# Weight conversions pinned behind a layer's stores, copies and maxima, with loads two units ahead

## The chip, the cores and the metric

The kernel runs on one core of a Trainium2 chip. The metric is device time in microseconds (us). Engines are named as in the profile: PE multiplies matrices (PEld is its weight load), DVE, ACT and POOL are the vector, scalar and general engines, and SP issues all transfers (its queue is SPq in the trace). Each engine takes its instructions in the order in which they stand in its queue.

## The reference

The program chains three parts over 2304 tokens (4 batches of 576): attention with a decay mask and no softmax, a feed-forward layer whose hidden value is the maximum of three products, and a gated one.

```python
rel = pos[:, None] - pos[None, :]
Dmat = np.where(rel >= 0, gamma[:, None, None] ** rel[None, :, :], 0.0)
x = np.matmul(scale * np.matmul(q, k.transpose(0, 1, 3, 2)) * Dmat, v)   # 4 x 8 heads, 576, 64
x = x.transpose(0, 2, 1, 3).reshape(2304, 512)
h = np.maximum(np.maximum(x @ w1, x @ w2), x @ w3)                       # 2304 x 768
y = h @ w_out                                                           # 2304 x 512
g = y @ w_gate                                                          # 2304 x 1536
out = (g * (1.0 / (1.0 + np.exp(-g))) * (y @ w_val)) @ w_out2           # 2304 x 512
```

q, k and v are float32. The weights arrive as 64-bit floats, which the kernel reads as pairs of 32-bit words and converts itself.

## The kernel before

**The main loop.** Lines 329 to 350 run 32 steps (n = 0 to 31), one for each batch, half sequence and pair of heads. A step loads the attention input of step n + 4 (`a_load`, L139 and L147, twelve transfers in later steps), finishes the attention of step n (`a_value`: the matmuls at L230 and L233, the copy L236 on ACT, the subtraction L237 on DVE), and prepares the next ones (`a_state`, `a_score`, `a_prep`, which transposes the loaded tile qk on DVE at L174 and L175). From step 4 on it also works on slices of the first feed-forward layer: `f_some` takes slices off a list, three in steps up to 8 and five from step 9 on.

**A slice** (`f_slice`) is twelve matmuls (L298) into a PSUM tile of 288 columns, of which there are two (`ps_mm`). Three slices belong to one block of h: the first is copied out by ACT (L302), the second and third are combined into it by DVE (the maxima, L304), and after the third SP stores the block to memory (L306, h_d).

**The conversions.** The 18 weight units of the first layer are converted in steps 1 to 8 (`win_conv`). The other weights, 42 units of 128 x 512, are converted from step 9 on by `spill`: SP loads a unit (`load_w`, 512 KB; L97 or L99; three buffers w), ACT takes both words (L106, L107), DVE puts them together (L108, L109, L110), and SP stores the result as float32 (L285, wd). The code calls `spill` once in each step from 9 on and a second time in steps 12, 16, 20, 24 and 28, that is 28 times, then 6 times in the loop at L382 (which finishes the slices of the last block and splits w_out into high and low parts, `wo_load`, and h, `h_split`), and 8 times in the loop at L456, which computes y = h w_out (matmuls L473, drained by L478 or L482). What needs the other weights, from L556 on, reads them from memory (`w_ops`, `p_ops`).

**What sets the order.** PE's instructions stand in the order of the code (`manual_schedule`). For ACT, DVE, POOL and SP a scheduler builds the queues: it goes through a simulated time line and puts in front what it holds ready first, so that a conversion, which depends only on its load and its buffers, may come many steps ahead of its place in the code. SP issues its transfers round-robin on eight semaphores, and a transfer waits until the one eight places before it has landed.

```python
        sp_load(i)
        sp_load(i + 1)
        l = conv32(sp_ld.pop(i))
```

Of the kernel before, what the change touches and what calls it, by code (L numbers as in the profile page):

```python
# [13 lines left out]
ACTF = mybir.ActivationFunctionType  # L14
ALU = mybir.AluOpType
# [47 lines left out]
def retention_moe(ctx, tc, consts, q, k, v, w1, w2, w3, w_out, w_gate, w_val, w_out2, out):  # L63
    nc = tc.nc
    pe, act, dve, pool, sp = nc.tensor, nc.scalar, nc.vector, nc.gpsimd, nc.sync

    def f(ap):
        return ap.bitcast(F32)

    dram = ctx.enter_context(tc.tile_pool(name="dram", bufs=1, space=DRAM))  # L70
    h_d = [dram.tile([F1, P, TOK[i][1]], F32, name=f"h_d{i}", tag=f"h_d{i}") for i in range(NHB)]
# [22 lines left out]
    def load_w(src):  # L94
        t = stg.tile([P, 512], U64, name="w64", tag="w64")
        if len(src.shape) == 3:
            sp.dma_start(out=t.rearrange("p (a b) -> p a b", a=src.shape[1]), in_=src)  # L97
        else:
            sp.dma_start(out=t, in_=src)  # L99
        return t  # L100

    def conv32(t):
        u = t.bitcast(U32).rearrange("p (n two) -> p n two", two=2)
        z = stg.tile([P, 512], U32, name="wz", tag="wz", bufs=2)
        l = stg.tile([P, 512], U32, name="wl", tag="wl")
        act.activation(f(z), f(u[:, :, 1]), ACTF.Copy, scale=float(2.0 ** -112))  # L106
        act.activation(l, u[:, :, 0], ACTF.Copy, scale=float(2.0 ** -29))  # L107
        dve.tensor_scalar(z, z, 3, None, ALU.logical_shift_left)  # L108
        dve.scalar_tensor_tensor(z, u[:, :, 1], 0x80000000, z, ALU.bitwise_and, ALU.bitwise_or)  # L109
        dve.tensor_tensor(l, z, l, ALU.add)  # L110
        return f(l)
# [16 lines left out]
    def a_load(n):  # L128
        if n >= NU:
            return  # L130
        b, h, pr = units[n]
        c0 = h * C
        u = {}
        for nm, s in (("k", k), ("q", q), ("v", v)):
            if nm == "q" and n >= PT:
                continue
            u[nm] = att.tile([CK, NC, 2, D], F32, name=f"{nm}n", tag=f"{nm}n", bufs=4)
            for e in range(2):
                sp.dma_start(out=u[nm][:, :, e, :],  # L139
                             in_=s[b, 2 * pr + e, c0:c0 + C].rearrange("(a p) d -> p a d", p=CK))  # L140
        if n >= PT:
            u["t"] = att.tile([P, 2, C // 32, 32], F32, name="qk", tag="qk", bufs=3)
            for i, s in enumerate((k, q)):
                for e in range(2):
                    for x in range(2):
                        g = 64 * e + 32 * x
                        sp.dma_start(out=u["t"][g:g + 32, i],  # L147
                                     in_=s[b, 2 * pr + e, c0:c0 + C, 32 * x:32 * x + 32].rearrange("(a p) d -> p a d", p=32))
        U[n] = u
# [71 lines left out]
    def a_value(n):  # L221
        b, h, pr = units[n]
        u = U.pop(n)
        z = stz[n % 3]
        o = psa.tile([P, C], F32, name="o_ps", tag="o_ps")
        for c in range(NC):
            for e in range(2):
                oc = o[64 * e:64 * e + 64, c * CK:(c + 1) * CK]
                if c or h:
                    pe.matmul(oc, z[:, c, e], u["qg"][:, c], start=c == 1 - h, stop=False, skip_group_check=True)  # L230
        for c in range(NC):
            for e in range(2):
                pe.matmul(o[64 * e:64 * e + 64, c * CK:(c + 1) * CK], u["v"][:, c, e], u["pT"][:, e, c],  # L233
                          start=False, stop=True, skip_group_check=True)
        xh, xl = [ffn.tile([P, C], F32R, name=f"x{x}", tag=f"x{x}{pr}", bufs=3) for x in "hl"]
        act.activation(xh, o, ACTF.Copy)  # L236
        dve.tensor_tensor(xl, o, f(xh), ALU.subtract)  # L237
        xs[(2 * b + h, pr)] = (xh, xl)
# [11 lines left out]
    def win_conv(i):  # L250
        if i >= len(win_units):
            return
        if i not in win_ld:
            win_load(i)
        win_load(i + 1)
        hi = ffn.tile([P, 512], F32R, name="wh", tag=f"wh{i}")
        lo = ffn.tile([P, 512], F32R, name="wlo", tag=f"wlo{i}")
        l = conv32(win_ld.pop(i))
        act.activation(hi, l, ACTF.Copy)
        pool.tensor_tensor(lo, l, f(hi), ALU.subtract)  # L260
        w_in[win_units[i]] = (hi, lo)


    sp_units = [(("o", fi), w_out[fi * P:fi * P + P, :]) for fi in range(F1)]
# [4 lines left out]
    sp_ld = {}  # L269
    sp_n = [0]  # L270

    def sp_load(i):
        if i < len(sp_units) and i not in sp_ld:
            sp_ld[i] = load_w(sp_units[i][1])

    def spill():
        i = sp_n[0]
        if i >= len(sp_units):
            return
        sp_n[0] += 1  # L280
        sp_load(i)
        sp_load(i + 1)
        l = conv32(sp_ld.pop(i))
        wd[sp_units[i][0]] = t = dram.tile([P, 512], F32, name=f"wd{i}", tag=f"wd{i}")
        sp.dma_start(out=t, in_=l)  # L285

    mx = {}

    def f_slice(hb, fi, wi):
        wh, wl = w_in[(fi, wi)]  # L290
        cw = TOK[hb][1]
        ps = ps_mm.tile([P, C], F32, name="ps", tag="mm")[:, 0:cw]
        n = 0
        for kc in range(KD):
            xh, xl = xs[(hb, kc)]
            ksl = slice(kc * P, kc * P + P)
            for l, r in ((wh, xl), (wl, xh), (wh, xh)):
                pe.matmul(ps, l[:, ksl], r, start=n == 0, stop=n == 3 * KD - 1)  # L298
                n += 1
        if wi == 0:  # L300
            mx[hb] = ffn.tile([P, C], F32, name="hmax", tag="hmax", bufs=3)[:, 0:cw]
            act.activation(mx[hb], ps, ACTF.Copy)  # L302
        else:
            dve.tensor_tensor(mx[hb], ps, mx[hb], ALU.max)  # L304
        if wi == 2:
            sp.dma_start(out=h_d[hb][fi], in_=mx[hb])  # L306

    fq = []

    def f_some(n):  # L310
        for _ in range(n):
            if fq:
                f_slice(*fq.pop(0))
# [15 lines left out]
    for n in range(NU):  # L329
        if n % NP == 0 and n:  # L330
            fq += [(n // NP - 1, fi, wi) for fi in range(F1) for wi in range(3)]
        a_load(n + 4)
        a_value(n)
        a_state(n + 1)
        a_score(n + 1)
        quota, ncv = ((2, 3) if n >= 9 else (1, 2)), 0
        if 1 <= n < 4:
            ncv = 1
        elif 4 <= n < 9:
            ncv = 3  # L340
        for _ in range(min(ncv, len(win_units) - wc)):
            win_conv(wc)
            wc += 1
        if n >= 9:
            spill()
            if n % 4 == 0:
                spill()
        f_some(quota[0])
        a_prep(n + 2)
        f_some(quota[1])  # L350
    pe_order.__exit__(None, None, None)
    psa_cm.__exit__(None, None, None)
    att_cm.__exit__(None, None, None)
# [99 lines left out]
        W[(nm, k)] = (hi, lo)  # L453


    for o in range(NHB):  # L456
        hb = order2[o]
        sb, blk, side = hb // 4, hb % 2, (hb // 2) % 2
        if sb == 0:
            if side == 0:  # L460
                x_tiles(blk)
                sc = [scratch() for j in range(KH)]
        else:
            st2 = wr.tile([P, 7, C], F32, name="sf", tag="sf")
        for e in (0, 2, 1, 3):
            ps = ps_mm.tile([P, C], F32, name="ps2", tag="mm")
            n = 0
            for fi in range(F1):
                wh, wl = wo[fi]
                hh, hl = hsp[(o, fi)]  # L470
                es = slice(e * P, e * P + P)
                for l, r in ((wh, hl), (wl, hh), (wh, hh)):
                    pe.matmul(ps, l[:, es], r, start=n == 0, stop=n == 3 * F1 - 1)  # L473
                    n += 1
            j, kh = e % KH, e // KH
            if sb == 0:
                sf, b12 = sc[j]
                act.activation(b12 if side and not kh else sf[:, 2 * side * kh + (1 - side) * kh], ps, ACTF.Copy)  # L478
                if side and kh:
                    x_ops(blk, j, sf, b12)  # L480
            else:
                act.activation(st2[:, e], ps, ACTF.Copy)  # L482
            for fi in ((0, 1), (3, 4), (2,), (5,))[e]:
                h_split(o + 1, fi)
        spill()
        if sb:
            x2d[hb] = t = dram.tile([P, KD, C], F32, name=f"x2d{hb}", tag=f"x2d{hb}")
            sp.dma_start(out=t, in_=st2[:, 0:KD])
            if o == NHB - 4:
                w_ops("g", 0)  # L490
            elif o == NHB - 3:
                w_ops("v", 0)
# [183 lines left out]
```

## Time and profile before

| | us |
|---|---|
| median of 3 runs | 928.68 (928.52 to 929.08) |
| the profiled execution | 926.66 |
| its span in the trace | 924.9 |
| PE busy in the span | 835.0 (90%) |
| DVE, ACT, POOL busy | 560.1, 398.1, 314.8 |
| first to last matmul of the first layer (L298) | 46.8 to 398.9 |
| first conversion to last (L106) | 11.7 to 282.9 |

The profiled execution is one run with the profiler; durations and waits come from it. In a list of groups the columns are: line, engine, operation, output<-inputs, count | busy time, mean ns of one | idle time of the engine just before them, and what ended it. In a list of waits: the waiting engine and line, the one it waited for, total, times, longest.

### The profile page before, as it was taken

What the parts mean: (1) busy time and instruction counts of PE and PEld (TensorE: products, weight loads), DVE (VectorE), ACT (ScalarE), POOL (GpSimd) and SP (SyncE); (2) the same over time, 40 slices, a digit from 0 to 9 for tenths busy, and PEclk for the clock granted to TensorE, in tenths of its full rate; (3) what the DMA queues carried; (4) which work ended last, traced back from release to release, by engine and by line L of the source; (5) the groups of instructions that cost most, each with busy time, mean ns of one, the idle gap of its engine ahead of it and who ended that gap; (6) DMA issues with size and microseconds to landing.
All of it is one profiled execution on the core that took longest, in us unless ns stands there. A gap on an engine that the chain in (4) does not pass through costs nothing.

```text
span 924.9 us, 17315 instructions
## 1 busy us (share of the span) xinstructions
PE 835.0 (90%) x6424; PEld 780.9 (84%) x6424; DVE 560.1 (61%) x1092; ACT 398.1 (43%) x916; POOL 314.8 (34%) x345
## 2 busy tenths in 40 slices
PE   5577788888788999999998999999998999999998
PEld 4477687787788999899887999989987899989997
DVE  3688667676675443326426647766699557566644
ACT  3565344344343122236535553444445654534431
POOL 3244100000000000113435655646636556456431
PEclk9589999999999999999997999999999999999999
DMA  7887788878886212312534112112124221020003
GB/s 175 199 223 185 185 225 249 227 222 256 251 228 173 63 33 81 118 52 83 154 125 129 42 28 69 41 29 66 49 78 130 91 69 43 28 59 22 1 2 102
DMA packets 170340, 105.99 MB, mean 115 GB/s; under 512 B 107664, under 2 KB 155792, under 8 KB 170256
## 3 DMA queue, kind: packets, MB, share of 16 engines
q1 hardware_dynamic: 170256, 104.89, 40.9%
q8 instruction: 50, 0.82, 0.4%
q14 instruction: 34, 0.28, 0.1%
HBM read 79.68 MB, written 25.17 MB: 113 GB/s over the span
## 4 chain that ended last, share of the span: by engine, by line
PE 38%; DVE 6%; DMA 3%; issue 2%; POOL 1%; ACT 1%; SPq 0%; DVEq 0%; POOLq 0%
PE ps L533 13%; PE g L556 12%; PE v L556 12%; DMA sf<-wd 2%; DVE sg L601 1%; PE ps L473 1%; DMA hf<-h_d 1%; DVE acc L539 1%; DVE sf L443 1%; DVE t L618 1%; DVE sf L445 0%; POOL wl L450 0%; DMA sf<-x2d 0%; DVE t L584 0%; DMA x2d<-sf 0%
## 5 line engine op out<-in xcount | busy, mean ns | idle before, releaser
L298 PE MATMUL ps<-xl,wh 128*128 128x288 f32 x576 | 179.5, 312 | 47.3 <-ACT hmax L302 25.4
L298 PE MATMUL ps<-xh,wh 128*128 128x288 f32 x576 | 172.6, 300 | 0.0
L298 PE MATMUL ps<-xh,wlo 128*128 128x288 f32 x576 | 172.2, 299 | 0.0
L298 PEld LDWEIGHTS ps<-xl,wh 128*128 128x128 f32 x576 | 110.7, 192 | 57.8 <-ACT hmax L302 28.9
L298 PEld LDWEIGHTS ps<-xh,wlo 128*128 128x128 f32 x576 | 111.2, 193 | 0.0
L298 PEld LDWEIGHTS ps<-xh,wh 128*128 128x128 f32 x576 | 111.1, 193 | 0.0
L556 PE MATMUL g<-xl,wh 128*128 128x288 f32 x336 | 101.2, 301 | 6.9 <-DVE sg L601 3.0
L160 POOL TENSOR_TENSOR ks<-kn,cst 96x384 f32<-96x384 f32 (+1 forms) x32 | 26.2, 818 | 233.8 <-PE m_ps L205 143.7
L556 PE MATMUL g<-xh,wl 128*128 128x288 f32 x336 | 100.4, 299 | 0.5 <-POOL wl L447 0.5
L556 PE MATMUL v<-xl,wh 128*128 128x288 f32 x336 | 99.7, 297 | 1.1 <-DVE t L588 1.1
L556 PE MATMUL g<-xh,wh 128*128 128x288 f32 x336 | 99.9, 297 | 0.0
L556 PE MATMUL v<-xh,wl 128*128 128x288 f32 x336 | 99.4, 296 | 0.2 <-POOL wl L447 0.2
L556 PE MATMUL v<-xh,wh 128*128 128x288 f32 x336 | 99.3, 295 | 0.0
L627 POOL TENSOR_TENSOR gl<-t,gh 128x288 fp32r<-128x288 f32 (+1 forms) x72 | 54.8, 761 | 109.8 <-ACT gh L626 78.1
L304 DVE TENSOR_TENSOR hmax<-ps,hmax 128x288 f32<-128x288 f32 x96 | 43.0, 448 | 60.1 <-PE ps L298 51.8
L539 DVE TENSOR_TENSOR acc<-ps,acc 128x512 f32<-128x512 f32 x90 | 61.8, 687 | 28.4 <-PE ps L533 28.4
L533 PE MATMUL ps<-ph,gl 128*128 128x512 f32 x192 | 75.4, 393 | 2.3 <-DVE acc L539 2.3
L106 ACT ACTIVATE wz<-w 128x512 f32<-128x512 f32 x60 | 40.4, 673 | 85.7 <-DMA w<-in_moe_w_val_dram 29.6
L533 PE MATMUL ps<-ph,gh 128*128 128x512 f32 x192 | 75.8, 395 | 0.0
L533 PE MATMUL ps<-pl,gh 128*128 128x512 f32 x192 | 75.1, 391 | 0.0
L556 PEld LDWEIGHTS g<-xl,wh 128*128 128x128 f32 x336 | 64.2, 191 | 9.9 <-DVE sg L601 3.3
L556 PEld LDWEIGHTS g<-xh,wl 128*128 128x128 f32 x336 | 64.4, 192 | 2.7 <-POOL wl L447 0.7
(113 smaller groups left out, 2003.7 us busy)
## 6 DMA issues: line engine op xcount, KB each, us to landing
wd<-wl SPq DMA_DIRECT2D x42, 256.0 KB, 3.6
w<-in_moe_w_dram SPq DMA_DIRECT2D x18, 512.0 KB, 4.9
w<-in_moe_w_out_dram SPq DMA_DIRECT2D x18, 512.0 KB, 6.0
h_d<-hmax SPq DMA_DIRECT2D x48, 144.0 KB, 2.4
hf<-h_d SPq DMA_DIRECT2D x48, 144.0 KB, 2.4
w<-in_moe_w_gate_dram SPq DMA_DIRECT2D x12, 512.0 KB, 5.1
w<-in_moe_w_val_dram SPq DMA_DIRECT2D x12, 512.0 KB, 5.8
sf<-wd SPq DMA_DIRECT2D x24, 256.0 KB, 3.1
```

The source lines that it names most:

```text
L106: act.activation(f(z), f(u[:, :, 1]), ACTF.Copy, scale=float(2.0 ** -112))
L160: pool.tensor_tensor(u["ks"][:, 0:nk], u["k"][:, 0:nk], sc, ALU.mult)
L298: pe.matmul(ps, l[:, ksl], r, start=n == 0, stop=n == 3 * KD - 1)
L304: dve.tensor_tensor(mx[hb], ps, mx[hb], ALU.max)
L443: dve.tensor_tensor(q[4], a21, q[2], ALU.add)
L473: pe.matmul(ps, l[:, es], r, start=n == 0, stop=n == 3 * F1 - 1)
L533: pe.matmul(ps, l, r, start=n == 0, stop=n == 5)
L539: dve.tensor_tensor(acc[s], ps, acc[s], ALU.add)
L556: pe.matmul(bank, w[l][:, a, js], x[r][:, i, j], start=start and n == 0, stop=stop and n == 3 * KH - 1, skip_group_check=True)
L601: dve.tensor_tensor(t, c, t, ALU.mult)
L618: dve.tensor_tensor(o, c, t, ALU.mult)
L627: pool.tensor_tensor(gl, o[:, c0:c1], f(gh), ALU.subtract)
```

## The change

Three things change. The last copy (ACT), the last maximum (DVE) and the last h_d store (SP) that the code has issued are remembered in `pace`; a conversion's instructions on ACT and DVE, and a load's transfer on SP, must stand behind them in their queues (`issue_after` sets an order on one engine and adds no wait). In `spill` the load of the next unit is called behind the conversion, and the one after next too, so loads are two units ahead. In a step, the call of `spill` stands behind the first two slices, and the second call at the step's end. Before the loop at L456 `pace` is emptied, so its eight conversions are pinned to nothing.

```diff
+    pace = {}
+
+    def paced(*names):
+
+        st = ExitStack()
+        for nm in names:
+            if nm in pace:
+                st.enter_context(tc.issue_after(pace[nm]))
+        return st
+
     def sp_load(i):
         if i < len(sp_units) and i not in sp_ld:
-            sp_ld[i] = load_w(sp_units[i][1])
+            with paced("sp"):
+                sp_ld[i] = load_w(sp_units[i][1])
...
         sp_load(i)
+        with paced("act", "dve"):
+            l = conv32(sp_ld.pop(i))
         sp_load(i + 1)
-        l = conv32(sp_ld.pop(i))
+        sp_load(i + 2)
...
-            act.activation(mx[hb], ps, ACTF.Copy)
+            pace["act"] = act.activation(mx[hb], ps, ACTF.Copy).ins
...
-            dve.tensor_tensor(mx[hb], ps, mx[hb], ALU.max)
+            pace["dve"] = dve.tensor_tensor(mx[hb], ps, mx[hb], ALU.max).ins
...
-            sp.dma_start(out=h_d[hb][fi], in_=mx[hb])
+            pace["sp"] = sp.dma_start(out=h_d[hb][fi], in_=mx[hb]).ins
...
+        f_some(quota[0])
         if n >= 9:
             spill()
-            if n % 4 == 0:
-                spill()
-        f_some(quota[0])
         a_prep(n + 2)
         f_some(quota[1])
+        if n >= 9 and n % 4 == 0:
+            spill()
...
+    pace.clear()
     for o in range(NHB):
```

Lines 302, 304 and 306 of the kernel before are 315, 317 and 319 in the changed one, and 285, 377 and 478 are 298, 390 and 492. The queues of PE and POOL keep their order.

ACT's queue before, at steps 11 and 12 (hmax<-ps is the copy, xh<-o_ps and stz<-st belong to attention; the number behind w names the unit's buffer):

```order
L302 ACTIVATE hmax<-ps 128x288
L106 ACTIVATE wz<-w_2089 128x512
L107 ACTIVATE wl<-w_2089 128x512
L236 ACTIVATE xh<-o_ps 128x288
L106 ACTIVATE wz<-w_2233 128x512
L107 ACTIVATE wl<-w_2233 128x512
L219 ACTIVATE stz_82<-st 64x3x64 x2
L106 ACTIVATE wz<-w_2244 128x512
L107 ACTIVATE wl<-w_2244 128x512
L302 ACTIVATE hmax<-ps 128x288
```

Three conversions stand between one copy and the next. The same engine in the changed kernel, at steps 13 and 14:

```order
L315 ACTIVATE hmax<-ps 128x288
L106 ACTIVATE wz<-w_1543 128x512
L107 ACTIVATE wl<-w_1543 128x512
L236 ACTIVATE xh<-o_ps 128x288
L219 ACTIVATE stz_83<-st 64x3x64 x2
L315 ACTIVATE hmax<-ps 128x288
L106 ACTIVATE wz<-w_1685 128x512
L107 ACTIVATE wl<-w_1685 128x512
L315 ACTIVATE hmax<-ps 128x288
```

Each conversion now stands directly behind a copy, one between two copies. SP's queue in the changed kernel at the same place (qk, kn and vn are attention loads, h_d the blocks of h, w a weight load, wd a converted weight on its way out):

```order
L319 DMA h_d_58<-hmax 128x288
L99 DMA w_1543<-in_moe_w_out_dram 128x512
L147 DMA qk<-in_q_dram 32x9x32 x2
L298 DMA wd_1545<-wl 128x512
L147 DMA qk<-in_q_dram 32x9x32
L319 DMA h_d_58<-hmax 128x288
L99 DMA w_1685<-in_moe_w_out_dram 128x512
```

A weight load now stands directly behind an h_d store; counted over the whole queue, three to four h_d stores lie between a load and its conversion, where it was one or two. Before, weight loads and stores came in bunches between h_d stores:

```order
L306 DMA h_d_58<-hmax 128x288
L97 DMA w_2533<-in_moe_w_gate_dram 128x4x128
L285 DMA wd_2542<-wl 128x512
L97 DMA w_2673<-in_moe_w_gate_dram 128x4x128
L97 DMA w_2816<-in_moe_w_val_dram 128x4x128
L139 DMA vn<-in_v_dram 96x3x64 x2
```

Behind the main loop ACT's queue had no conversions. In the changed kernel, from the last copy into the first output block (sf<-ps are its drains):

```order
L315 ACTIVATE hmax<-ps 128x288
L106 ACTIVATE wz<-w_4724 128x512
L107 ACTIVATE wl<-w_4724 128x512
L106 ACTIVATE wz<-w_4908 128x512
L106 ACTIVATE wz<-w_5055 128x512
L107 ACTIVATE wl<-w_4908 128x512
L107 ACTIVATE wl<-w_5055 128x512
L492 ACTIVATE sf<-ps_4785 128x288
L492 ACTIVATE sf<-ps_4817 128x288
L106 ACTIVATE wz<-w_5188 128x512
L107 ACTIVATE wl<-w_5188 128x512
L492 ACTIVATE sf<-ps_4843 128x288
```

The last eight conversions moved in among the drains, and on DVE among the splits of h (hl).

## Rows read from the trace of the kernel before

**Rows 1.** The page: the span, and PE's busy tenths in 40 slices.
```profile
span 924.9 us, 17315 instructions
...
PE   5577788888788999999998999999998999999998
```

**Rows 2.** Stretches, L233 alone: start:end, length, busy (count) PE and PEld, clock, DMA.
```profile
97.10:304.10 207.00, 10.67 (x192) 8.95 (x194) 0.98 0.82 224
304.10:324.40 20.30, 1.33 (x24) 1.12 (x26) 1.00 0.24 56
341.60:361.90 20.30, 1.33 (x24) 1.11 (x24) 1.00 0.07 23
```

**Rows 3.** Waits of PE, 97.1 to 304.1.
```profile
PE ps L298 <- DVE hmax L304: 21.1, 15, 3.4
PE ps L298 <- ACT hmax L302: 13.2, 9, 4.3
```

**Rows 4.** Groups by line, ACT, 97.1 to 304.1.
```profile
L106 ACT ACTIVATE wz<-w 128x512 f32<-128x512 f32 x41 | 27.5, 672 | 64.7 <-DMA w<-in_moe_w_val_dram 29.6 <-DMA w<-in_moe_w_gate_dram 18.9 <-DMA w<-in_moe_w_out_dram 14.2
L107 ACT ACTIVATE wl<-w 128x512 uint32<-128x512 uint32 x41 | 27.4, 668 | 4.9 <-DMA wd<-wl 4.2 <-DMA w<-in_moe_w_out_dram 0.4
```

**Rows 5.** Groups by line, DVE, 97.1 to 304.1.
```profile
L110 DVE CUSTOM_DVE_ANT_0 wl<-wz,wl 128x1024 uint16<-128x1024 uint16 x42 | 29.8, 709 | 2.4 <-ACT wl L107 0.5
L109 DVE SCALAR_TENSOR_TENSOR wz<-w,wz 128x512 uint32<-128x512 uint32 x42 | 28.8, 686 | 0.8
L304 DVE TENSOR_TENSOR hmax<-ps,hmax 128x288 f32<-128x288 f32 x55 | 24.4, 445 | 13.9 <-PE ps L298 10.0 <-issue 2.0 <-DMA h_d<-hmax 1.5
L108 DVE TENSOR_SCALAR wz<-wz 128x512 uint32<-128x512 uint32 x41 | 18.0, 440 | 33.5 <-ACT wz L106 33.2
...
L175 DVE STREAM_TRANSPOSE qt<-qk 128x288 f32<-128x288 f32 x17 | 8.0, 471 | 19.0 <-DMA qk<-in_q_dram 15.4 <-DMA w<-in_moe_w_out_dram 3.5
```

**Rows 6.** Instructions in order of time, 143.3 to 148.2: start, length, engine, line.
```profile
143.29 0.29 PE L298 MATMUL ps<-xh,wh 128*128 128x288 f32 x1
...
144.40 0.66 ACT L106 ACTIVATE wz<-w 128x512 f32<-128x512 f32 x1 [4.61 <-DMA w<-in_moe_w_val_dram]
...
147.39 0.40 ACT L302 ACTIVATE hmax<-ps 128x288 f32<-128x288 f32 x1
147.84 0.57 PE L298 MATMUL ps<-xl,wh 128*128 128x288 f32 x1 [4.25 <-ACT hmax L302]
```

**Rows 7.** Stretches, busy PE, PEld, DVE, ACT, POOL, clock, DMA: steps 9, 10, 13; behind.
```profile
97.10:114.60 17.50, 12.17 (x109) 11.39 (x106) 10.92 (x24) 5.58 (x12) 0.91 (x2) 0.90 0.82 203
114.60:126.10 11.50, 10.72 (x110) 9.93 (x106) 8.92 (x19) 5.38 (x12) 0.61 (x1) 1.00 0.80 216
...
154.80:164.90 10.10, 10.10 (x109) 9.78 (x106) 8.74 (x20) 5.50 (x11) 0.82 (x1) 1.00 0.85 238
...
361.90:399.00 37.10, 34.83 (x272) 34.00 (x269) 11.90 (x25) 10.07 (x23) 4.72 (x5) 1.00 0.38 119
399.00:418.00 19.00, 19.00 (x145) 19.00 (x144) 6.98 (x12) 8.55 (x19) 3.13 (x4) 1.00 0.19 56
```

**Rows 8.** Instructions in order of time, PE within a slice.
```profile
131.23 0.30 PE L298 MATMUL ps<-xh,wh 128*128 128x288 f32 x1
131.36 0.29 PE L298 MATMUL ps<-xl,wh 128*128 128x288 f32 x1
```

**Rows 9.** Instructions in order of time: a wait of DVE, then SP's queue.
```profile
296.66 0.48 DVE L175 STREAM_TRANSPOSE qt<-qk 128x288 f32<-128x288 f32 x1 [3.22 <-DMA qk<-in_q_dram]
...
299.06 1.81 SPq L147 DMA_DIRECT2D qk<-in_k_dram  x4
300.91 1.95 SPq L147 DMA_DIRECT2D qk<-in_q_dram  x4
```

**Rows 10.** The page: transfers, count, KB each, median us from issue to landing.
```profile
w<-in_moe_w_out_dram SPq DMA_DIRECT2D x18, 512.0 KB, 6.0
...
w<-in_moe_w_gate_dram SPq DMA_DIRECT2D x12, 512.0 KB, 5.1
```

## The prediction

> **What bounds the kernel now.** I read the page first: PE is 90% busy over a span of 924.9 us, and its busy tenths fall below 9 in the first third [rows 1]. Then I cut the span by steps of the main loop. Every step issues twelve matmuls at L233, so counting these in stretches counts steps. From 97.1 to 304.1 there are 192 of them, 16 steps (9 to 24) in 207.0 us, 12.94 us a step; from 304.1 to 324.4 and from 341.6 to 361.9 there are 24 each, two steps in 20.3 us, 10.15 us a step, with the same five slices of first-layer work in a step [rows 2]. At the later pace the 16 steps would take 162.4 us. So 44.6 us are lost in that stretch: 34.3 us is PE waiting for a copy or a maximum that empties a PSUM tile (21.1 for DVE, 13.2 for ACT) [rows 3], the other 10 us are what surrounds such a wait: the first matmul after it is slower, and the granted clock was 0.90 in one stretch with long waits, a mean of its two levels, 2.4 and 1.2 GHz [rows 7].
>
> Who holds ACT and DVE? In that stretch ACT runs 41 conversions (L106) and stands idle 64.7 us in front of them, for weights that are not there yet; DVE stands 33.5 us in front of L108, behind the same ACT instruction [rows 4, 5]. Both engines take their instructions in order. One wait shows the chain: PE ends a slice at 143.6; ACT has been waiting 4.61 us for a weight load and begins L106 at 144.40; two conversions and the state copy later the copy L302 runs at 147.39, and PE goes on at 147.84, after 4.25 us [rows 6]. The conversions themselves are not the price: step 13 ran 10.1 us with PE busy throughout, though ACT was 5.5 us and DVE 8.74 us busy in it; step 10 was 11.5 us with as much [rows 7]. Three conversions began in each.
>
> **The change, part by part.** The instructions are the same: 42 loads, conversions and stores, the same PE order. What moves is when.
>
> (a) Conversions of steps 9 to 31 now stand behind the last copy on ACT and the last maximum on DVE: 28 in 23 steps (1.22 a step) instead of 41 in 16 (2.56 a step). A load now stands three to four h_d stores ahead of its conversion instead of one or two. Five slices a step, three for one store, put a store about 6 us apart at 10.15 us a step, so the load has some 18 us for its 5.1 to 6.0 us to landing [rows 10] and the wait of [rows 6] has no cause. Removed: at most the whole excess, -44.6 us.
>
> (b) Step 9 itself was 17.5 us [rows 7], 7.35 over. Its first-layer weights still come late, since the nine steps before are unchanged; the three early conversions in it go. Bounds 0 and 7.35; I keep 3.
>
> (c) Steps 10 to 27 (18 steps) must carry their part of the conversions, and they load for attention. Here the queue of SP is what can come next. A step now issues 12 attention loads, 1.67 stores of h_d and 2.43 transfers of weights, 16.1 in all. Before it was 18.8 in 12.94 us, 0.69 us each, waits included; eight attention loads with no weights among them took 1.81 + 1.95 = 3.76 us, 0.47 each [rows 9]. So 16.1 of them need between 7.6 and 11.1 us of a step of 10.15: the bounds are 0 and 0.95 us a step. The attention loads are no further ahead than before (one h_d store ahead of their transpose in both orders), and DVE stood 19.0 us in front of the transpose L175, 1.19 a step [rows 5]. I take 0.6 a step, close to the mean loss of steps 10 and 13 (1.35 and 0) and between the two queue bounds: 18 x 0.6 = +10.8 us.
>
> (d) Steps 28 to 31 had no conversions and now get some five, with no attention loads any more. Bounds 0 and 5 x 1.09, where 1.09 us is 44.6 / 41, the price of a conversion so far; I take 0.3 a step, +1.2.
>
> (e) Fourteen conversions land after the main loop, between the last slices and the first output blocks, where none were. From 361.9 to 418 ACT is busy 18.6 and DVE 18.9 of 56.1 us [rows 7]. A conversion costs ACT 1.34 us and DVE 0.44 + 0.69 + 0.71 = 1.84 us [rows 4, 5], so fourteen bring ACT to 37.4 and DVE to 44.7 us, 80%, less than the 87% of step 13. They fit on average. But the last eight are pinned to nothing and stand in a row ahead of the drains of the first output block and of the splits of the second one, with loads of 512 KB straight in front of them. Bounds 0 and 14 x 1.09 = 15.3; I take a third, +5, because PE there has 18 matmuls to a drain instead of 12.
>
> Sum: -44.6 + 3 + 10.8 + 1.2 + 5 = -24.6 us. The second half (from 449.6 on) reads the converted weights long after they are stored and keeps its order; I put it at nothing. The profiled execution took 926.66 us, so 902.1; the median of the runs is 2.0 us above it, hence **904 us**.
>
> **The edge of the pinned order.** A slice is 12 matmuls 0.13 us apart [rows 8], 1.6 us. With two PSUM tiles a maximum may start 1.6 - 0.45 = 1.15 us late, less a hand-over, before PE stops. DVE now runs maximum, L108, L109, maximum: 0.45 + 0.44 + 0.69 = 1.58 us, just inside a slice, if L106 on ACT is in time.
>
> The Trainium skill (DMA: Bandwidth & Descriptors, Queues, rings and completion order) says that each DMA engine takes descriptors in ring order. By that rule a weight load issued earlier stands in front of the attention loads issued behind it on the same ring, and pulling loads ahead does not shorten the wait for those. One row agrees: the trace puts 3.5 us of DVE's wait at L175, out of 19.0, to a load of w_out [rows 5]. By the rule the sum would be that of the second rival below, by the row alone that of (c).
>
> **Rivals.**
> 1. *Nearly all comes back.* Step 13 is the pattern: loads in, no loss. Then (c), (d) are 0, (b) is 3, (e) is 2: -39.6, 889 us. For it: 1.22 conversions a step are less than half of step 13's three. Against: the SP queue at 16.1 issues a step. Chance 0.17.
> 2. *The attention loads stay late.* The transposes still wait 1.2 us a step in front of the maxima, 18 x 1.2 = 21.6, and in the end (e) costs 10: -44.6 + 3 + 21.6 + 1.2 + 10 = -8.8, 920 us. For it: the wait of 3.22 us at 296.66, when the weights were almost done [rows 9], and the unchanged lead. Against: steps 25 and 26 without loss. Chance 0.13.
> 3. *Slower: a pinned conversion always falls in front of a maximum.* If L106 comes late on ACT, L108 holds DVE and each of the 42 conversions delays a maximum by L108 + L109, 1.13 us, at no slack. 42 x 1.13 = 47.5, -44.6 + 47.5 = +2.9, 931.6 us; with half of (e)'s upper bound on top 939. It decides where the delay passes the 1.15 us of the edge above, that is if a load takes over some 18 us or ACT is 0.1 us late each time. Against: ACT is idle most of a step. Chance 0.08.
> 4. *Nothing:* the excess moves whole to the places (c) and (e), within 0.2%. Chance 0.05.
>
> **How the numbers follow.** The forecast, gains of 15 to 33 us, has 0.57. The likeliest is its 904. Taking in rival 1 and rival 2 up to its price gives 888 to 920; outside are rivals 3 and 4, half of rival 2 and a little below, some 2 in 10. About 0.2% (1.9 us) is what a measurement here tells from no change. Faster: 0.57 + 0.17 + 0.13 = 0.87; same 0.05; slower 0.08.
>
> **What would show it.** In the profile of the changed kernel: idle time of ACT in front of L106 for weight loads falls from 64.7 to under 10 us in steps 9 to 24, and DVE's in front of L108 with it (a); PE's waits for the copy and the maximum there fall from 34.3 to about 10 us; steps 10 to 27 take 10.5 to 11 us; rival 1 would show 10.2, rival 2 long waits of DVE at L175 for qk; after the main loop PE shows waits of some 5 us for the copies, the drains or the splits (e). I am wrong if waits for weight loads stay, for then loads are not early on the chip, or if the stretch from the end of the main loop to the first output blocks grows by more than 10 us.

## The result, and the profile after

| | before | after |
|---|---|---|
| median of 4 runs, us | 928.60 (925.91 to 929.08) | 901.08 (898.39 to 904.19) |
| ratio | 1 | 0.9711, 95% interval 0.967 to 0.9751 |
| the profiled execution / its span, us | 926.66 / 924.9 | 902.81 / 901.0 |
| steps 9 to 24, us | 207.0 | 171.3 |
| the seam (step 31 to the last first-layer matmul), us | 36.9 | 36.3 |
| first output block to first gate matmul (L570), us | 50.6 | 62.9 |

The forecast was 904.0 for the median and 902.1 for the profiled execution. The first layer's last matmul moved from 398.9 to 361.2 us (-37.7). From the first output block to the first gate matmul 12.3 us were given back, behind it 1.4. The page of the changed kernel, its span and PE's row of tenths:

```profile
span 901.0 us, 17296 instructions
...
PE   6578899999999999879979999999998999999998
...
```

Against [rows 1] the shallow third between tenths 7 and 8 is full; a new dent stands in slices 17 and 18, from 360 to 405 us. The same cut by steps as in [rows 2], L233 alone (start:end, length, busy and count of PE and PEld, clock, DMA):

```profile
95.70:267.00 171.30, 10.67 (x192) 8.93 (x192) 1.00 0.69 172
267.00:287.30 20.30, 1.33 (x24) 1.12 (x24) 1.00 0.66 182
304.60:324.90 20.30, 1.33 (x24) 1.12 (x24) 1.00 0.43 138
```

Sixteen steps at 10.7 us each in this execution, where 10.15 is the pace of a step that loses nothing. Waits of PE in 95.7 to 267.0, answering [rows 3]:

```profile
PE ps L311 <- DVE hmax L317: 4.1, 5, 1.7
PE ps L311 <- ACT hmax L315: 2.0, 2, 1.2
```

34.3 us have become 6.1. Groups by line in the same stretch, ACT and then DVE, answering [rows 4, 5]:

```profile
L106 ACT ACTIVATE wz<-w 128x512 f32<-128x512 f32 x20 | 13.4, 671 | 4.0 <-DMA w<-in_moe_w_out_dram 3.7
```

```profile
L175 DVE STREAM_TRANSPOSE qt<-qk 128x288 f32<-128x288 f32 x16 | 7.6, 478 | 22.5 <-DMA qk<-in_q_dram 19.5 <-DMA w<-in_moe_w_out_dram 3.0
L108 DVE TENSOR_SCALAR wz<-wz 128x512 uint32<-128x512 uint32 x19 | 8.0, 421 | 11.0 <-ACT wz L106 10.8
```

ACT's idle time in front of a conversion fell from 64.7 to 4.0 us. DVE's in front of L108 fell from 33.5 to 11.0, and what is left there ends with ACT's own L106. The wait in front of the transpose L175 did not fall: 1.4 us a step, 1.19 before.

The new dent: stretches of the changed kernel with busy time of PE, PEld, DVE, ACT and POOL, from the seam through output blocks 0, 1, 2:

```profile
325.00:361.40 36.40, 34.78 (x271) 33.97 (x268) 26.35 (x49) 18.82 (x39) 5.32 (x5) 1.00 0.82 265
361.40:373.40 12.00, 9.84 (x74) 9.61 (x74) 7.71 (x14) 6.42 (x12) 0.00 (x0) 1.00 0.98 308
373.40:385.40 12.00, 10.14 (x74) 9.54 (x73) 9.65 (x16) 8.24 (x18) 3.03 (x3) 1.00 0.68 237
385.40:402.60 17.20, 11.93 (x73) 11.23 (x73) 7.65 (x15) 7.60 (x17) 7.23 (x4) 0.90 0.20 59
```

A block took 9.5 us before (399.0 to 418.0 in [rows 7] are two of them). These take 12.0, 12.0 and 17.2. In the third PE is also busy 2 us longer for the same work: the granted clock was 0.90 there, a mean of its two levels 2.4 and 1.2 GHz, after two waits of 2.43 and 2.49 us. The seam in front, with its six conversions, is no longer than before. Waits of PE from 361 to 426:

```profile
PE ps L487 <- ACT sf L492: 5.0, 3, 2.5
PE ps L487 <- POOL hl L391: 4.0, 2, 2.4
```

Two instances, first the drain L492 in order of time (ACT, then PE; start, length, engine, line):

```profile
366.21 0.66 ACT L106 ACTIVATE wz<-w 128x512 f32<-128x512 f32 x1 [1.42 <-DMA w<-in_moe_w_gate_dram]
366.89 1.24 ACT L107 ACTIVATE wl<-w 128x512 uint32<-128x512 uint32 x2
368.02 0.71 ACT L492 ACTIVATE sf<-ps 128x288 f32<-128x288 f32 x2
```

```profile
368.48 0.40 PE L487 MATMUL ps<-hl,woh 128*128 128x288 f32 x1 [2.16 <-ACT sf L492]
```

This is the picture of [rows 6], moved: an unpinned conversion waits on ACT for its load, and the drain for which PE waits stands behind it. The other kind is POOL's split of h:

```profile
386.59 4.84 POOL L391 TENSOR_TENSOR hl<-hf,hh 128x288 fp32r<-128x288 f32 x1 [3.38 <-ACT hh L390]
```

```profile
391.48 0.41 PE L487 MATMUL ps<-hl,woh 128*128 128x288 f32 x1 [2.43 <-POOL hl L391]
```

A split that takes 0.8 us on POOL took 4.84 here; the section on the hardware comes back to it.

### The profile page after: what moved, and what is told of

It is laid out like the page before. It is cut to its first block, busy times and chain, and to the rows that moved or that the text cites. A ratio compares the mean times of both kernels' runs of the same rounds, so it can differ in the third digit from the quotient of the medians.

```text
span 901.0 us, 17296 instructions
## 1 busy us (share of the span) xinstructions
PE 833.3 (92%) x6424; PEld 781.1 (87%) x6424; DVE 563.5 (63%) x1092; ACT 395.0 (44%) x916; POOL 317.4 (35%) x345
## 4 chain that ended last, share of the span: by engine, by line
PE 38%; DVE 6%; DMA 3%; issue 2%; POOL 2%; ACT 2%; SPq 1%; DVEq 0%; POOLq 0%; ACTq 0%
PE ps L547 14%; PE g L570 12%; PE v L570 12%; DMA sf<-wd 2%; DVE sg L615 1%; DVE acc L553 1%; DVE t L632 1%; DVE sf L456 1%; PE ps L487 1%; POOL wl L463 1%; DVE sf L458 0%; DVE t L598 0%; DMA sf<-x2d 0%; DVE sf L459 0%; DMA hf<-h_d 0%
## 5 line engine op out<-in xcount | busy, mean ns | idle before, releaser
L311 PE MATMUL ps<-xl,wh 128*128 128x288 f32 x576 | 175.8, 305 | 16.6 <-ACT hmax L315 10.8
L311 PE MATMUL ps<-xh,wh 128*128 128x288 f32 x576 | 171.3, 297 | 0.0
L570 PE MATMUL g<-xl,wh 128*128 128x288 f32 x336 | 101.2, 301 | 4.8 <-DVE sg L615 2.0
L570 PE MATMUL v<-xl,wh 128*128 128x288 f32 x336 | 100.1, 298 | 1.1 <-DVE t L602 1.1
L570 PE MATMUL g<-xh,wl 128*128 128x288 f32 x336 | 100.4, 299 | 0.5 <-POOL wl L460 0.5
L570 PE MATMUL g<-xh,wh 128*128 128x288 f32 x336 | 100.0, 298 | 0.0
L570 PE MATMUL v<-xh,wl 128*128 128x288 f32 x336 | 99.7, 297 | 0.0
L570 PE MATMUL v<-xh,wh 128*128 128x288 f32 x336 | 99.6, 296 | 0.0
L570 PEld LDWEIGHTS g<-xl,wh 128*128 128x128 f32 x336 | 64.3, 191 | 7.7 <-DVE sg L615 2.2
L487 PE MATMUL ps<-hl,woh 128*128 128x288 f32 x192 | 58.5, 305 | 11.5 <-ACT sf L492 5.0
L391 POOL TENSOR_TENSOR hl<-hf,hh 128x288 fp32r<-128x288 f32 x24 | 27.2, 1135 | 116.0 <-ACT hh L390 113.3
```

The costliest lines, as they stand in the source:

```text
L391: (pool, dve)[fi % 2].tensor_tensor(hl, hf, f(hh), ALU.subtract)
L570: pe.matmul(bank, w[l][:, a, js], x[r][:, i, j], start=start and n == 0, stop=stop and n == 3 * KH - 1, skip_group_check=True)
```

## Experiments

The kernel before ran beside each; a ratio is to its runs on the same chip (medians 932.3 to 932.6 us). Edits are against the changed kernel unless something else is said. Times of a stretch are those of one profiled execution, and two executions of the same queues can differ: in e7_pin_blocks and e8_hl_dve, whose edits lie behind the main loop, ACT, DVE, POOL and SP have the changed kernel's instructions in its order up to 300 us, and steps 9 to 24 took 179.7 and 175.8 us, with 11.1 and 9.2 us of PE's waits there, where the changed kernel's took 171.3 with 6.1. So a difference of 8 us in this stretch is not yet an effect of an edit.

**Which part makes the gain?**

```diff
-            if nm in pace:
+            if nm in pace and nm == "none":
```

> The changed kernel without the pins: calls of spill where the change has them, loads two ahead, but nothing has to stand behind a copy, a maximum or a store. Theory (the pins make the order, the scheduler pulls the rest ahead as before): conversions end by step 23, ACT waits in front of L106 again, 922 to 930 us. Rival (the loads being two ahead is what removes the waits): about 905 us.

Measured: 930.71 us, ratio 0.9996 (0.9968 to 1.0025); steps 9 to 24 took 211.6 us. Row of ACT's groups and waits of PE in its steps 9 to 24:

```profile
L106 ACT ACTIVATE wz<-w 128x512 f32<-128x512 f32 x41 | 27.6, 672 | 74.1 <-DMA w<-in_moe_w_out_dram 32.3 <-DMA w<-in_moe_w_val_dram 23.5 <-DMA w<-in_moe_w_gate_dram 13.8
```

```profile
PE ps L311 <- DVE hmax L317: 20.0, 10, 4.2
PE ps L311 <- ACT hmax L315: 12.0, 6, 3.3
```

Without the pins all 41 conversions are back in these steps, and the waits of [rows 3, 4] with them, though the calls stand at their new places. The whole gain hangs on the pins. No run keeps the pins with the calls at their old places, or pins one engine alone, so which pin carries it stays open. The lead of the loads was tried from both ends. One unit ahead, pins kept:

```diff
         sp_load(i + 1)
-        sp_load(i + 2)
```

> The changed kernel with loads one unit ahead, pins kept. A unit comes every 8 us, so a load still has 6 to 8 us for its 5 to 6 us to landing. Theory: nearly all stays, 901 to 907 us, with some waits of ACT for loads. Rival (two ahead is needed): waits of 1 to 3 us for most loads, 28 x 1 us or more, 915 us and above.

Measured: 905.84 us, ratio 0.9734 (0.9693 to 0.9775); steps 9 to 24 took 178.2 us, ACT stood 14.1 us in front of L106 there (4.0 in the changed kernel). Two units ahead in the kernel before, without pins:

```diff
         sp_load(i + 1)
         l = conv32(sp_ld.pop(i))
+        sp_load(i + 2)
```

> The kernel before with one line added: the load after next is called behind the conversion. Theory: the order of SP and ACT stays bunched, the three buffers and SP's queue limit the loads and not the call, 925 to 930 us. Rival (loads too late in the code are the cause): under 915 us.

Measured: 934.17 us, ratio 1.0021 (0.999 to 1.0053). So two ahead shows no gain alone and at most some us with the pins: the interval of e3_one_ahead overlaps with that of the changed kernel, and 178.2 us lies within what the changed kernel's own queues took.

**Where does the given-back part come from?** The theory: from the eight conversions in the blocks. All 42 into the main loop, pinned, 1.8 a step:

```diff
-        if n >= 9 and n % 4 == 0:
+        if 9 <= n < 28:
             spill()
```

> All 42 conversions are pinned within the main loop: the second call of spill comes in every step from 9 to 27, so 41 stand in steps 9 to 31 (1.8 a step) and none stands among the output blocks. Theory (the eight unpinned conversions cost the first output blocks 12.4 us; the main loop has room): the first four output blocks start 9.6 us apart again, the last slice ends 2 to 4 us later than in the changed kernel (361.4), total about 891 us. Rival (a conversion over 1.2 a step costs its old price of 1.09 us): the main loop loses 14 x 1.09 = 15 us, total about 904.

Measured: 924.93 us, ratio 0.9915 (0.9885 to 0.9944), so both expectations missed. Its first blocks:

```profile
400.30:409.90 9.60, 9.60 (x74) 9.60 (x73) 1.38 (x3) 2.48 (x6) 0.81 (x1) 1.00 0.05 17
409.90:419.40 9.50, 9.50 (x74) 9.50 (x73) 5.72 (x10) 6.08 (x13) 2.45 (x3) 1.00 0.34 94
```

The blocks are whole again, 50.6 us to the gate: the 12.3 us do come from the conversions there. But the main loop lost more than that, 200.7 us in steps 9 to 24 (171.3 in the changed kernel) and 63.4 in 25 to 30 (57.9). Steps 9 to 24, L233 alone, then the group of the transpose and the waits of PE there:

```profile
99.40:300.10 200.70, 10.67 (x192) 8.91 (x194) 0.95 0.74 194
```

```profile
L175 DVE STREAM_TRANSPOSE qt<-qk 128x288 f32<-128x288 f32 x16 | 7.6, 472 | 27.0 <-DMA qk<-in_q_dram 21.3 <-DMA kn<-in_k_dram 5.4 <-DVE wz L109 0.3
```

```profile
PE ps L311 <- DVE hmax L317: 24.7, 10, 5.2
```

The longest of these waits, in order of time (DVE, SP's queue, PE):

```profile
230.78 0.48 DVE L175 STREAM_TRANSPOSE qt<-qk 128x288 f32<-128x288 f32 x1 [5.37 <-DMA kn<-in_k_dram]
231.19 0.65 DVE L110 CUSTOM_DVE_ANT_0 wl<-wz,wl 128x1024 uint16<-128x1024 uint16 x1
...
233.00 0.41 DVE L317 TENSOR_TENSOR hmax<-ps,hmax 128x288 f32<-128x288 f32 x1
```

```profile
224.97 0.45 SPq L97 DMA_DIRECT2D w<-in_moe_w_val_dram  x1
225.47 2.16 SPq L147 DMA_DIRECT2D qk<-in_q_dram  x1
...
228.76 0.90 SPq L139 DMA_DIRECT2D kn<-in_k_dram  x2
231.91 0.34 SPq L298 DMA_DIRECT2D wd<-wl  x1
233.10 0.31 SPq L147 DMA_DIRECT2D qk<-in_k_dram  x1
```

```profile
233.47 0.61 PE L311 MATMUL ps<-xl,wh 128*128 128x288 f32 x1 [5.21 <-DVE hmax L317]
```

Two queues hold each other here. DVE stands 5.37 us in front of a transpose for an attention load. The row names kn, but the transpose reads qk, and kn landed at 231.2, when the transpose had begun. The last piece of qk is the one: SP issued it at 225.47, directly behind a weight load of 512 KB, and it landed at 230.61, the weight load at 230.42. Behind the transpose stand L110 and the maximum. SP's store of the converted weight cannot go before L110 has run (231.91), and the next attention load stands behind that store (233.10).

So attention loads share SP's queue with two things that can hold them: stores that wait for DVE, and weight loads in front. The second can be counted. In e1_spread, steps 9 to 24, the last piece of qk was issued directly behind a weight load in 8 of 16 transposes, and these have 18.4 of the 27.0 us of DVE's wait; in the changed kernel it is 1 of 16, with 1.9 of 22.5 us. Three tests took transfers out of SP's queue.

The stores away from SP, on e1_spread:

```diff
-        sp.dma_start(out=t, in_=l)
+        pool.dma_start(out=t, in_=l)
```

> The spread version of the first experiment (1.8 conversions a step), with the 42 stores of converted weights issued from POOL's queue instead of SP's. There SP issued 17.3 transfers a step in 12.5 us, 0.72 us each; in the changed kernel 16.1 in 10.7, 0.67 each; before 18.8 in 12.9, 0.69 each. Theory (SP's queue sets the step): 15.5 transfers at 0.67 to 0.72 give 10.4 to 11.2 us a step instead of 12.5, the first layer ends 20 to 30 us earlier than in the spread version, total 895 to 905 us. Rival (the conversions on DVE or the transfer engines are the limit, not the issuing): same transfers and conversions, so steps stay at 12.5, 920 us or more.

Measured: 915.76 us, ratio 0.9829 (0.9757 to 0.9902); steps 9 to 24 took 190.6 us. Less than expected: by the profiles a third of the loss in these steps, with 23.2 us of waits in front of L175 still there, and the intervals of the two ratios overlap. The same edit on the changed kernel:

> The changed kernel with the stores of converted weights issued from POOL. SP issues 14.9 transfers a step instead of 16.1. Theory (SP's queue): the 6.9 us that steps 10 to 24 still lose fall to under 3; the output blocks, where SP also held stores and h loads in one queue, lose a little less than 12.4; total 892 to 899 us. Rival: within 2 us of the changed kernel, 899 to 903.

Measured: 900.90 us, ratio 0.9654 (0.9602 to 0.9705), an interval that overlaps with the changed kernel's; steps 9 to 24 took 174.1 us, the first block to the gate 57.7 (62.9).

The attention loads away from SP, on e1_spread (L139 and L147):

```diff
-                sp.dma_start(out=u[nm][:, :, e, :],
+                pool.dma_start(out=u[nm][:, :, e, :],
...
-                        sp.dma_start(out=u["t"][g:g + 32, i],
+                        pool.dma_start(out=u["t"][g:g + 32, i],
```

> e1_spread with the attention loads (kn, qn, vn, qk; L139 and L147) issued from POOL's queue in place of SP's. Theory (queues hold each other: SP's h_d and wd stores wait for DVE, the attention loads queued behind them go out late, and DVE's queue then stands in front of the transposes that need those loads, with the maxima behind them): DVE's waits for qk, kn and qn fall from about 31 us in steps 9 to 24 to under 10, the waits of TensorE for maxima from 28 us to under 10, steps 9 to 24 take 170 to 180 us (200.7 in e1_spread), the output blocks stay 9.6 us apart, and the time is 885 to 900. Rival (1.8 conversions a step are simply too much work in order on ScalarE and VectorE): steps 9 to 24 stay above 193 us and the time at 915 to 927 whatever queue the loads use. A third way: the loads behind POOL's k scaling go out later than before, and the time is above 927.

Measured: 907.27 us, ratio 0.9722 (0.969 to 0.9754). The mechanism came as expected (steps 9 to 24 174.6 us, no wait in front of L175), the time did not: step 9 began at 107.3 us, 11.5 later than in the changed kernel. So the early loads went back to SP:

```diff
+        ld, u = (pool if n >= 13 else sp), {}
...
-                pool.dma_start(out=u[nm][:, :, e, :],
+                ld.dma_start(out=u[nm][:, :, e, :],
```

> e9_spread_attn_pool, but only the attention loads of units 13 and up (written at steps 9 and up) are issued from POOL's queue; those before stay on SP. e9_spread_attn_pool took 174.6 us for steps 9 to 24 with no wait of VectorE for qk, but reached step 9 at 107.3 us in place of 95.8 (the changed kernel), as its early loads stood behind POOL's work. If that is the price of its early loads: step 9 at 95 to 99 us, steps 9 to 24 at 172 to 177, output blocks 9.6 us apart, first gate matmul at 416 to 421 us, time 891 to 898 (e9_spread_attn_pool 907.3 less 9 to 12, with 2 to either side). Rival (the late start only moved a wait that the spread brings anyway, step 9's 14.5 us among it): step 9 starts early but steps 9 to 24 take 180 to 187, time 901 to 908.

Measured: 895.04 us (894.22 to 898.14), ratio 0.9615 (0.9576 to 0.9653). Steps 9 to 24, the transpose and the waits of PE there:

```profile
98.10:272.00 173.90, 11.18 (x192) 9.42 (x194) 0.98 0.77 222
```

```profile
L175 DVE STREAM_TRANSPOSE qt<-qk 128x288 f32<-128x288 f32 x15 | 7.0, 468 | 1.6 <-DMA qk<-in_k_dram 1.6
```

```profile
PE ps L311 <- DVE hmax L317: 6.5, 5, 2.9
```

All 42 conversions stand in the main loop as in e1_spread, and steps 9 to 24 take 26.8 us less. That settles what e1_spread lost: not the engines' work, but the queue that attention loads share with stores and weight loads. The loads now go out earlier: the last piece of qk was issued 11.0 us (median) before its transpose, 4.5 in e1_spread. Whether the stores' waiting, the weight loads in front or SP's issue time weighs most stays open, since the loads leave all three; no run takes the weight loads alone out of SP's queue. The first gate matmul is at 420.7 us (424.3), the blocks begin 9.5 to 10.1 us apart.

Between the two rates, every other step in place of every fourth, loads on SP:

```diff
-        if n >= 9 and n % 4 == 0:
+        if n >= 9 and n % 2 == 0:
             spill()
```

> The changed kernel with its second call at every other step (n even) in place of every fourth: 33 conversions in the main loop (1.5 a step), six in the seam, three in the blocks. Between 28 (the changed kernel, 901) and 42 (e1_spread, 925). If the loss in the main loop grows in proportion to the conversions a step: steps 9 to 24 at 183 to 188 us (171 and 201 at the ends), the blocks about 7 us shorter than the changed kernel's 62.9, time 903 to 909. If there is slack for 1.5 a step and the loss sets in only above it: steps 9 to 24 at 170 to 176 us, time 892 to 897.

Measured: 897.88 us (893.38 to 900.66), ratio 0.9616 (0.9584 to 0.9648). Steps 9 to 24 took 179.3 us, between the two expectations and within what the changed kernel's own queues took, so whether the loss sets in at this rate stays open; the first block to the gate took 51.3 us. The transpose in steps 9 to 24:

```profile
L175 DVE STREAM_TRANSPOSE qt<-qk 128x288 f32<-128x288 f32 x16 | 7.6, 477 | 21.3 <-DMA qk<-in_q_dram 21.3
```

By its calls this kernel has 34 conversions in the loop (the expectation counts 33). Set side by side, with 28, 34 and 42 DVE stood 22.5, 21.3 and 27.0 us in front of L175, and PE waited 6.1, 10.7 and 27.3 us for copies and maxima. The first two are not told apart, for with 28 PE waited up to 11.1 us in another execution. From 34 to 42 DVE's wait grows by a quarter, and what PE loses more than doubles.

**What in the blocks?** The last eight pinned too, two each in blocks 0, 2, 4 and 6, behind drains, splits and loads of h:

```diff
+            d = sp.dma_start(out=hf, in_=h_d[i][fi])
+            if o:
+                pace["sp"] = d.ins
...
+                pace["act"] = act.activation(st2[:, e], ps, ACTF.Copy).ins
...
-        spill()
+            if o % 2 == 0 and e >= 2:
+                spill()
```

> The changed kernel with the last eight conversions pinned as well: two in each of output blocks 0, 2, 4 and 6, behind the second and fourth drain on ACT, the last split on DVE and the last load of h on SP. Theory (the eight cost 12.4 us because they stand in a row in the first block in front of drains and splits): blocks 0 to 3 start 9.6 to 10.2 us apart instead of 12.0, 12.0, 17.2 and 9.6, total 888 to 893 us. Rival (eight conversions cost about 1.5 us each wherever they stand in the blocks, by DVE's and POOL's time): the loss spreads over eight blocks, total 898 to 903.

Measured: 904.85 us, ratio 0.9705 (0.9645 to 0.9765); the first block to the gate took 60.4 us (62.9). The theory that the missing pins make the loss fell: waits of PE for ACT's drains fell to 2.0 us, but waits for POOL's splits grew to 5.4. All splits on DVE, pins as in the changed kernel:

```diff
-            (pool, dve)[fi % 2].tensor_tensor(hl, hf, f(hh), ALU.subtract)
+            dve.tensor_tensor(hl, hf, f(hh), ALU.subtract)
```

> The changed kernel with all splits of h (hl) on DVE, none on POOL. In the changed kernel one split on POOL took 4.84 us instead of 0.8 while DVE ran its sums from SBUF, and PE waited 4.0 us for two such splits. Theory (POOL is held up by DVE's work on SBUF, and this is a part of the 12.4 us): PE's waits for POOL vanish, DVE gets 24 x 0.46 us more, total 896 to 900 us. Rival (DVE is the one that is late; giving it more makes it worse): 903 to 910.

Measured: 898.76 us, ratio 0.9644 (0.9583 to 0.9704). Waits of PE from 361 to 426:

```profile
PE ps L311 <- DVE hmax L317: 3.6, 1, 3.6
PE ps L487 <- ACT s L492: 1.5, 1, 1.5
```

The waits for POOL are gone and the first block to the gate takes 54.3 us; but the seam grew from 36.3 to 42.1. The wait of 3.6 us there stands behind a pinned conversion: DVE stood 5.35 us in front of L108, for an L106 on ACT that had waited 4.50 us for its load. Whether the splits of block 0, now on DVE too, have a part in that is not shown. Both remedies, with block 0's splits left as they were:

```diff
-            (pool, dve)[fi % 2].tensor_tensor(hl, hf, f(hh), ALU.subtract)
+            (pool, dve)[1 if o else fi % 2].tensor_tensor(hl, hf, f(hh), ALU.subtract)
...
-        sp.dma_start(out=t, in_=l)
+        pool.dma_start(out=t, in_=l)
```

> The changed kernel with the 42 wd stores issued from POOL's queue (as in e6_after_poolst, 900.9) and the hl splits of blocks 1 to 7 all on VectorE (as in e8_hl_dve, 898.8, but not those of block 0, whose move had made the seam 42.1 us in place of 36.3). If the two gains are separate: seam 36 us, from block 0 to the first gate matmul 53 to 56 us (62.9 in the changed kernel), no wait of TensorE for POOL's hl, time 893 to 897. If VectorE's queue in the blocks carries the loss on in another form: 899 to 902, with waits for DVE's hl or for sf in the blocks of over 5 us.

Measured: 897.27 us (896.09 to 908.61), ratio 0.964 (0.9595 to 0.9686); seam 37.8, first block to gate 55.5 us. That is just above the 893 to 897 expected for separate gains.

e12_late_attn_pool and e11_every_other are faster than the changed kernel by about 1% of the ratio: their intervals end below 0.967, where its own begins. Between them and e10_poolst_hl the runs tell no difference.

## Why the prediction was right

Its place and, in the main, its mechanism were right, and its size came within 1 us of the profiled execution (902.1 forecast, 902.81) and 3 of the median. That closeness is luck: (e) was 6.7 us too low, (b) to (d) together came out 6.1 lower than put down, and the same queues took up to 8 us more for steps 9 to 24 in other executions.

- **(a)** held. The pins spread the conversions, the loads came in time, and the excess of 44.6 us went from steps 9 to 24 but for 8.9. e2_no_pins shows that the gain hangs on the pins. The lead of a load, put at some 18 us, was 16.4 us (median, from the issue of a load to its conversion in steps 9 to 24), 5.8 before; mostly one to three h_d stores went out in between, none or one before. It was more than was needed: in e3_one_ahead it was 7.2 us, and nearly all of the gain stayed.
- **(b)** step 9 kept 2.0 us (12.1 long), 3 were put down; in e7_pin_blocks it kept 6.0, in e8_hl_dve 4.2.
- **(c)** 10.8 us were put down for steps 10 to 27; steps 10 to 24 kept 6.9, steps 25 to 27 nothing. The suspicion was right, and the price is not shown to be wrong: in e7_pin_blocks and e8_hl_dve steps 10 to 24 kept 11.3 and 9.2. The wait in front of L175 stayed, as rival 2 said. What failed in rival 2 is the step from DVE's wait to PE's: 22.5 us of the one went with 6.1 us of the other (20.2 with 11.1 and 23.7 with 9.2 in those two runs), that is, at 1.2 conversions a step DVE's wait became PE's only in part. In e1_spread, where the rate is 1.8, 27.0 us went with 27.3.
- **The ring order.** The 3.5 us that were read as agreeing with it do not show it: the piece of qk that ended that wait was issued at 104.17, and the load of w_out only at 104.70. The changed kernel does show loads in front: in 15.9 of its 22.5 us in front of L175 a weight load issued ahead of the last piece was still under way, before in none.
- **(d)** 1.2 put down, nothing found.
- **(e)** is the term that was mis-sized: 5 put down, 11.7 measured (12.3 in the blocks less 0.6 in the seam), inside its bounds of 0 and 15.3. The first six conversions were free; all of it lies in the blocks with the eight that nothing pins, which the text named as the risk, though pinning them there (e7_pin_blocks) gave little of it back. The reason given for taking a third, 18 matmuls to a drain, did not hold: PE stood 2.16 us for one late drain all the same. A part of it, the 4.0 us for POOL's splits, was in no row the prediction had read.
- **Put at nothing**: step 9 began 1.4 us earlier, and the part behind the first gate matmul took 1.4 longer; the two cancel.
- **The edge of 1.58 us in a slice** did not bite: rival 3 did not come, with 6.1 us of waits in 16 steps.
- **The signs named**: ACT in front of L106 under 10 us (4.0); PE's waits about 10 (6.1); steps of 10.5 to 11 us (10.6 on average in steps 10 to 24); waits of about 5 us behind the main loop (10.0). The text called itself wrong if the stretch up to the first output blocks grew by more than 10 us; that stretch did not grow, but the blocks did, by 12.3. The sum survived because (b) to (d) came out lower.

## What to carry to other kernels

Background work that a scheduler may hoist can be pinned behind the short instructions that free PE's tiles; here nothing was gained without the pins, and the second unit of lead mattered little. What is left free gathers in front of the next stage's drains: pinned there it still cost 9.8 us of 12.3, moved into the loop it left the blocks whole. Before the rate is raised, look at which transfers share an in-order queue with weight loads and with stores that wait for the busy engine: at 42 conversions in the loop, other loads on another queue took 26.8 us off sixteen steps; at 34 the time was as good without that.

## What the runs showed of the hardware

**POOL beside VectorE.** In 24 splits of the changed kernel POOL took 0.79 us at least, 0.86 in the middle, 4.84 at most. Around the long one DVE ran sums and subtractions with both inputs in SBUF back to back, here its first and last:

```profile
386.55 0.75 DVE L427 TENSOR_TENSOR xl<-sf,xh 128x576 fp32r<-128x576 f32 x1
...
390.04 0.75 DVE L429 TENSOR_TENSOR xl<-sf,xh 128x576 fp32r<-128x576 f32 x1
```

DVE's chain ends at 390.79, POOL's split at 391.43, 0.64 us later. In e7_pin_blocks the same came again, DVE's chain ending at 394.19 and POOL's split at 394.85:

```profile
390.40 4.45 POOL L393 TENSOR_TENSOR hl<-hf,hh 128x288 fp32r<-128x288 f32 x1 [3.42 <-DVE xl L431]
```

```profile
393.45 0.74 DVE L433 TENSOR_TENSOR xl<-sf,xh 128x576 fp32r<-128x576 f32 x1
```

It looks as if POOL did its work only when DVE paused. The Trainium skill (SBUF — State Buffer, SBUF: two separate sides) says that the two engines share a pair of ports as an exclusive lock, which a DVE instruction with two SBUF inputs takes; these rows agree, and suggest that a chain of eight such instructions can keep POOL out for all of its length. No run here varied that by itself.

**Small transfers beside a weight load.** In steps 9 to 24 of the changed kernel a qk transfer of 36 KB that was issued while no weight load of 512 KB was under way landed after 2.0 us (median), with one under way after 3.8; in the kernel before it is 2.1 and 3.9, in e1_spread 2.1 and 4.0.

**Transfers issued by POOL.** In e12_late_attn_pool an attention transfer took POOL 0.61 us to issue and landed after 2.1, 4.4 and 7.2 us (least, median, most), in e1_spread from SP after 1.6, 3.3 and 5.7:

```profile
L147 POOL DMA_DIRECT2D qk<-in_k_dram x72: 607/612/772, 96.3 to 290.1; - x72
...
DMA to landing us min/median/max: 2.1/4.4/7.2
```

Each transfer is slower, and the transposes still stopped waiting for them: the last piece had landed 8.2 us (median) before its transpose, 0.1 us in e1_spread. When a load was issued counted for more here than how long it took.
